# Attention values with the value chunks stationary and four probability columns streaming, in steps of half a head

## The chip, the cores and the metric

The kernel runs on one core of a Trainium2 chip. The metric is the device time of one execution in microseconds (us). The time before is a median of 359.21 us over three runs (358.72 to 359.83). Ratios are computed as the mean time of one kernel's fast runs over the mean of the other's fast runs of the same rounds, so they are not quite the ratio of the medians quoted beside them. A run counts as slow when it is more than 1.5% above the fastest of the same kernel.

## The reference, cut to what matters

Two identical layers for four sequences (B = 4) at decode, so one new token each: an attention block with a cached key and value store of 4096 positions (32 query heads, 8 key/value heads, head size 128), then a gated feed-forward of width 1792.

```python
x = A_x
for _ in range(2):                                   # cut: written out twice in the reference
    h = layernorm(x)
    q = h @ wq                                       # 512 -> 32 heads x 128
    p = softmax(q k^T / sqrt(128))                   # 4 query heads share one key/value head
    x = x + (p v) @ wo
    h = layernorm(x)
    x = x + (gelu(h @ w_gate) * (h @ w_up)) @ w_down
```

The cache is 128 MiB in principle for two layers' worth of reads, but the transposed keys of one sequence stay on chip for both layers. What is loaded is 32 MiB of keys, twice 32 MiB of values, and 13.25 MiB of weights: 114.56 MB.

## The kernel before

For each sequence b, the kernel runs layer 1, and layer 2 up to the softmax. The value products of layer 2 ("the second pass") of sequence b - 1 are interleaved with the work of sequence b. Keys and values come through one ring of six 512 KB buffers, all issued from one queue in program order. A tile is half a head of keys or values.

```python
KV_BUFS = 6
kvin  = tc.tile_pool(name="kvin",  bufs=KV_BUFS)     # the ring, 4 KB per partition and buffer
prp   = tc.tile_pool(name="prp",   bufs=1)
ps_ot = tc.tile_pool(name="ps_ot", bufs=1, space=PSUM)
# ... cut

class Values:                                        # two heads at a time
    def step(self):                                  # half of two heads: two tiles
        # ... cut: two loads v_t into the ring
        for n in range(4):
            hi, k2 = n // 2, n % 2
            for i in range(2):                       # head
                for par in range(2):                 # four row groups of ot
                    kk = 2 * k2 + par
                    r = ZW * (2 * i + par)
                    c = ZW * (2 * (self.pp % 2) + i) + 2 * rep * kk
                    nc.tensor.matmul(self.ot[r:r + 2 * rep, 0],
                                     lhsT=self.pT[:, 2 * t + hi, c:c + 2 * rep],   # 8 columns stay
                                     rhs=vt[i][:, hi, 2 * kk:2 * kk + 2],          # 256 stream
                                     start=(t == 0 and n == 0), stop=(t == 1 and n == 3))
        if t == 1:
            nc.scalar.copy(out=self.os, in_=self.ot[:, 0])
    def finish(self):                                # fp32 selection: sum the wanted rows, transposed
        for k in range(2):
            nc.tensor.matmul(od, lhsT=self.os[:, k, :], rhs=sel[:, k], start=(k == 0), stop=(k == 1))
        nc.vector.tensor_tensor(out=o_bf[...], in0=od, in1=self.rden[...], op=ALU.mult)

# the end of sequence b; W() takes one step of the second pass of sequence b - 1
for n, _ in enumerate(ffn(b, 1)):                    # 3 x 56 pairs of one moving column
    if n > 0: W()
W()
run(layer_norm(b, 1, pad=True))
W()
qs = q_rows(b, 0)
W()
q_turn(qs, 0)
qs = q_rows(b, 1)
sc = scores(0, zq2)
q_turn(qs, 1)
soft2 = [softmax(sc), softmax(scores(1, zq2))]
W()
# then the keys of sequence b + 1
```

Of the kernel before, what the change touches and what calls it, by code (L numbers as in the profile page):

```python
# [1 line left out]

# [5 lines left out]
FP32 = mybir.dt.float32  # L8
BF16 = mybir.dt.bfloat16
I32 = mybir.dt.int32  # L10
ACT = mybir.ActivationFunctionType
ALU = mybir.AluOpType
AX = mybir.AxisListType
RED = bass_isa.ReduceOp
P = 128
# [3 lines left out]
GH = 4  # L19
# [5 lines left out]
def kernel(  # L25
# [41 lines left out]
    prp = ctx.enter_context(tc.tile_pool(name="prp", bufs=1))  # L67
    pTp = ctx.enter_context(tc.tile_pool(name="pTp", bufs=2 * NG))
    osp = ctx.enter_context(tc.tile_pool(name="osp", bufs=1))
# [4 lines left out]
    ps_ot = ctx.enter_context(tc.tile_pool(name="ps_ot", bufs=1, space=bass.MemoryType.PSUM))  # L74
# [20 lines left out]

    sel = const.tile([P, 2, 2, rep], FP32, name="sel")
    idv = ident_f.rearrange("p (s q b h) -> p q b s h", s=2, q=2, h=rep)
    for kbp in range(2):
        nc.vector.tensor_tensor(out=sel[:, kbp], in0=idv[:, 0, kbp], in1=idv[:, 1, kbp],
                                op=ALU.add)  # L100
# [33 lines left out]
    ot_ps = [ps_ot.tile([P, 2, 2 * Dh], FP32, name=f"ot{i}") for i in range(2)]  # L134
    for o in ot_ps:
        nc.vector.memset(o[:], 0.0)

# [96 lines left out]
    def run(gen):  # L234
        for _ in gen:
            pass

    def ffn(b0, nb):

        bs = slice(b0, b0 + nb)  # L240
        yield from layer_norm(b0, nb)
        yield
        h = ps_misc.tile([P, 2, KF, nb], FP32, name="h", tag="misc")
        rb = rstd[:, None, bs].to_broadcast([P, KF, nb])
        for m in range(KF):
            for k in range(KD):
                nc.tensor.matmul(h[:, 0, m, :], lhsT=wg_sb[:, k, m * P:(m + 1) * P],
                                 rhs=xc_bf[:, bs, k], start=(k == 0), stop=(k == KD - 1))
        g_sb = small.tile([P, KF, nb], FP32, name="g_sb", tag="g_sb")
        nc.vector.tensor_tensor(out=g_sb[:], in0=h[:, 0], in1=rb, op=ALU.mult)  # L250
        t1 = small.tile([P, KF, nb], FP32, name="t1", tag="t1")
        nc.vector.tensor_tensor(out=t1[:], in0=g_sb[:], in1=g_sb[:], op=ALU.mult)
        nc.vector.tensor_scalar(out=t1[:], in0=t1[:], scalar1=0.044715, scalar2=1.0,
                                op0=ALU.mult, op1=ALU.add)
        nc.vector.tensor_tensor(out=t1[:], in0=t1[:], in1=g_sb[:], op=ALU.mult)
        th = small.tile([P, KF, nb], FP32, name="th", tag="th")
        nc.scalar.activation(out=th[:], in_=t1[:], func=ACT.Tanh, scale=GELU_C)
        nc.vector.scalar_tensor_tensor(out=g_sb[:], in0=g_sb[:], scalar=0.5, in1=rb,
                                       op0=ALU.mult, op1=ALU.mult)
        nc.vector.scalar_tensor_tensor(out=th[:], in0=th[:], scalar=1.0, in1=g_sb[:],  # L260
                                       op0=ALU.add, op1=ALU.mult)
        yield
        for m in range(KF):
            for k in range(KD):
                nc.tensor.matmul(h[:, 1, m, :], lhsT=wu_sb[:, k, m * P:(m + 1) * P],  # L265
                                 rhs=xc_bf[:, bs, k], start=(k == 0), stop=(k == KD - 1))
        yield
        H_bf = small.tile([P, KF, nb], BF16, name="H_bf", tag="H_bf")
        nc.vector.tensor_tensor(out=H_bf[:], in0=th[:], in1=h[:, 1], op=ALU.mult)
        yT = ps_misc.tile([P, nb, KD], FP32, name="yT2", tag="misc")  # L270
        for dk in range(KD):
            for k in range(KF):
                nc.tensor.matmul(yT[:, :, dk], lhsT=wd_sb[:, k, dk * P:(dk + 1) * P],  # L273
                                 rhs=H_bf[:, k, :], start=(k == 0), stop=(k == KF - 1))
        nc.vector.tensor_tensor(out=XT[:, bs], in0=XT[:, bs], in1=yT[:], op=ALU.add)
# [76 lines left out]
    ot_ctr = [0]  # L352

    class Values:



        def __init__(self, b, pp, prob, o_bf):
            self.b, self.pp, self.o_bf = b, pp, o_bf
            self.pT, self.rden = prob  # L360
            self.ot = ot_ps[ot_ctr[0] % 2]
            ot_ctr[0] += 1
            self.t = 0

        def step(self):
            t = self.t
            self.t += 1
            vt = []
            for i in range(2):
                v = kvin.tile([P, 2, NKB, Dh], BF16, name="v_t", tag="kv")  # L370
                rows = slice(t * CH * P, (t + 1) * CH * P)
                dq.dma_start(out=v.rearrange("p i k d -> p (i k) d"),  # L372
                             in_=A_v_cache[self.b, 2 * self.pp + i, rows].rearrange(
                                 "(p c) d -> p c d", p=P))
                vt.append(v)
            for n in range(4):
                hi, k2 = n // 2, n % 2
                for i in range(2):
                    for par in range(2):
                        kk = 2 * k2 + par  # L380
                        r = ZW * (2 * i + par)
                        c = ZW * (2 * (self.pp % 2) + i) + 2 * rep * kk
                        nc.tensor.matmul(self.ot[r:r + 2 * rep, 0],  # L383
                                         lhsT=self.pT[:, 2 * t + hi, c:c + 2 * rep],
                                         rhs=vt[i][:, hi, 2 * kk:2 * kk + 2].rearrange(
                                             "p k d -> p (k d)"),
                                         start=(t == 0 and n == 0), stop=(t == 1 and n == 3),
                                         skip_group_check=True)
            if t == 1:
                self.os = osp.tile([P, 2, Dh], FP32, name="os", tag="os")  # L390
                nc.scalar.copy(out=self.os.rearrange("p b d -> p (b d)"), in_=self.ot[:, 0])  # L391

        def finish(self):
            od = self.ot[:, 1, 0:2 * rep]
            for k in range(2):
                nc.tensor.matmul(od, lhsT=self.os[:, k, :],  # L396
                                 rhs=sel[:, k].rearrange("p s h -> p (s h)"),
                                 start=(k == 0), stop=(k == 1))
            i0 = self.pp * 2 * rep
            s0 = 2 * (self.pp % 2)  # L400
            nc.vector.tensor_tensor(out=self.o_bf[:, self.b, i0:i0 + 2 * rep], in0=od,  # L401
                                    in1=self.rden[:, s0:s0 + 2].rearrange("p s h -> p (s h)"),
                                    op=ALU.mult)
# [20 lines left out]
    NPP = Hkv // 2  # L424

    def second_pass(b, probs):

        late = []
        for pp in range(NPP):
            v = Values(b, pp, probs[pp // 2], OT2_bf)  # L430
            for t in range(2):
                v.step()
                if late:
                    late.pop()()
                if t == 1:
                    late.append(v.finish)
                yield
        late.pop()()
        yield

    soft2 = prob2 = None
    for b in range(B):
# [3 lines left out]
        def W(n=1):  # L446
            for _ in range(n):
                next(todo, None)
# [11 lines left out]
        else:  # L460
# [3 lines left out]
            keys(b, 1)  # L464
            prob2.append(turn(soft2[1]))
            todo = second_pass(b - 1, prob2)
            keys(b, 2)
# [4 lines left out]
        p1 = turn(soft1)  # L472
        v = [Values(b, pp, p1, OT_bf) for pp in range(2)]
        v[0].step()
        keys(b, 6)
        v[0].step()
        keys(b, 7)
        v[1].step()
        soft1 = softmax(scores(1, z1))
        v[0].finish()  # L480
        if b == 0:
            dma_weights("wo")
        v[1].step()
        p1 = turn(soft1)
        v += [Values(b, pp, p1, OT_bf) for pp in range(2, 4)]
        v[2].step()
        v[1].finish()
        out_proj(b, 1, OT_bf, [0])
        v[2].step()
        out_proj(b, 1, OT_bf, [1, 2])  # L490
        v[3].step()
        v[2].finish()
        out_proj(b, 1, OT_bf, [3])
        v[3].step()
        if b == 0:
            dma_weights("wg", "wu", "wd")
        out_proj(b, 1, OT_bf, [4, 5])
        v[3].finish()
        W()
        out_proj(b, 1, OT_bf, [6, 7])  # L500
        W()
        for n, _ in enumerate(ffn(b, 1)):
            if n > 0:
                W()
        W()
        run(layer_norm(b, 1, pad=True))
        W()
        qs = q_rows(b, 0)
        W()
        q_turn(qs, 0)  # L510
        qs = q_rows(b, 1)
        sc = scores(0, zq2)
        q_turn(qs, 1)
        soft2 = [softmax(sc), softmax(scores(1, zq2))]
        W()
    prob2 = [turn(sf) for sf in soft2]
    todo = second_pass(B - 1, prob2)
    for n, _ in enumerate(todo):
        if n in (3, 5, 7):
            out_proj(0, B, OT2_bf, [n - 3, n - 2])  # L520
    out_proj(0, B, OT2_bf, [6, 7])
# [40 lines left out]
```

## Time and profile before

| | before |
|---|---|
| time, median of 3 | 359.21 us |
| mean load rate over the span | 322 GB/s |
| best slices of the span | 413 to 416 GB/s |
| PE busy | 272.8 us of 357.6 |

First lines of the page: the span, the busy time of each engine, the load rate in GB/s over 40 slices of 8.9 us, and the queue that brings instructions (packets, MB, share).

```profile
span 357.6 us, 10270 instructions
...
PE 272.8 (76%) x4548; PEld 197.1 (55%) x4548; DVE 124.2 (35%) x456; ACT 77.8 (22%) x122; POOL 13.4 (4%) x36
...
GB/s 286 416 416 277 356 356 394 416 396 396 88 169 323 344 406 384 374 376 369 161 312 345 413 400 387 386 380 191 298 359 395 351 369 393 345 265 140 405 47 2
...
q8 instruction: 35, 0.57, 0.6%
```

The rate touches 416 GB/s, but the slices that begin near 89, 170 and 241 us and the last ones fall well below it. The next view puts numbers on these stretches. Its columns are the stretch, the busy time and the instruction count of each engine, the granted clock, the DMA share and the rate.

```profile
core 0: us, PE busy (x) PEld busy (x) DVE busy (x) ACT busy (x) POOL busy (x), PEclk, DMA share, GB/s
90.00:110.00 20.00, 17.12 (x224) 10.59 (x217) 10.70 (x29) 6.78 (x10) 1.65 (x4) 0.82 0.42 149
165.00:190.00 25.00, 22.26 (x336) 15.02 (x329) 13.96 (x35) 10.00 (x14) 2.04 (x5) 0.92 0.77 277
240.00:265.00 25.00, 21.29 (x331) 15.64 (x331) 16.07 (x40) 11.31 (x16) 2.48 (x6) 0.99 0.79 280
312.00:328.00 16.00, 12.31 (x184) 6.36 (x176) 5.55 (x20) 2.30 (x6) 1.66 (x4) 0.82 0.53 194
```

These are the boundaries between sequences: feed-forward done, query rows, scores and softmax of layer 2, first keys of the next sequence. No tile of the ring is used up there for several microseconds, so the queue runs dry: after sequence 1 the last value step ends at 167.20 us and the key transposes begin at 174.32, and from 172 to 176 us the loads ran at 19 GB/s, a DMA share of 0.05.

The groups of the value products (line, engine, operation, tiles, shapes, count; then busy us and mean ns; then idle time before):

```profile
L383 PE MATMUL ot<-v_t,pT 128*8 128x256 bf16 x1024 | 69.1, 369 | 38.5 <-DMA v_t<-in_A_v_cache_dram 31.7
...
L391 ACT COPY os<-ot 128x256 f32<-128x256 f32 x32 | 11.9, 372 | 134.3 <-PE ot L383 134.3
...
L396 PE MATMUL ot<-sel,os 128*128 128x8 f32 x128 | 29.4, 340 | 0.0
```

The last fence of this section is the timeline of PE in a feed-forward stretch (start, duration, engine, line, what, count), and below it the sum of one such stretch, from the gate projection to the query rows of sequence 1, in the columns of the boundary table.

```profile
152.88 1.63 PE L247 MATMUL h<-xc_bf,wg_sb 128*128 128x1 bf16 x56
154.44 1.23 PE L383 MATMUL ot<-v_t,pT 128*8 128x256 bf16 x16
155.60 1.65 PE L265 MATMUL h<-xc_bf,wu_sb 128*128 128x1 bf16 x56
...
158.14 1.02 PE L396 MATMUL ot<-sel,os 128*128 128x8 f32 x4
```

```profile
153.00:164.50 11.50, 11.38 (x247) 8.60 (x248) 3.73 (x24) 0.96 (x3) 0.00 (x0) 0.50 1.02 380
```

PE is busy for 11.38 of 11.50 us there at a clock of 0.50. A pair step of values (L383 x16) takes about 1.0 us there, and so does a selection group (L396 x4).

### The profile page before, as it was taken

The numbers are of one execution on the slowest core, as the hardware profiler recorded it, in microseconds if no ns is written. First come the engines' busy times: TensorE is split into PE (matmuls) and PEld (weight loads), VectorE is DVE, ScalarE is ACT, GpSimd is POOL, SyncE is SP. The second block draws the span as 40 slices with busy tenths as digits, with TensorE's granted clock in tenths as the row PEclk, the third lists the DMA queues.
The fourth block names the chain that finished last, engine by engine and source line by source line (L and its number), as shares of the span: only waits on it lengthen the run. The fifth ranks groups of instructions, "written<-read, shape, count | busy, mean of one in ns | idle before, by whom it ended". The sixth has DMA issues, their size and how long they took to land.

```text
span 357.6 us, 10270 instructions
## 1 busy us (share of the span) xinstructions
PE 272.8 (76%) x4548; PEld 197.1 (55%) x4548; DVE 124.2 (35%) x456; ACT 77.8 (22%) x122; POOL 13.4 (4%) x36
## 2 busy tenths in 40 slices
PE   3777651964888588899887669998876797994785
PEld 3675540654266465584666546755665465742465
DVE  7235230031365430223666211336661203232013
ACT  2325220000055430000346210002562101011000
POOL 0000000000010000000100000001000000001000
PEclk9999885555599985555999975559998755587555
DMA  7997999999259999999489999995899999973910
GB/s 286 416 416 277 356 356 394 416 396 396 88 169 323 344 406 384 374 376 369 161 312 345 413 400 387 386 380 191 298 359 395 351 369 393 345 265 140 405 47 2
DMA packets 35740, 115.22 MB, mean 322 GB/s; under 512 B 3176, under 2 KB 9072, under 8 KB 35696
## 3 DMA queue, kind: packets, MB, share of 16 engines
q1 hardware_dynamic: 35696, 114.58, 85.2%
q8 instruction: 35, 0.57, 0.6%
q14 instruction: 9, 0.07, 0.1%
HBM read 114.56 MB, written 0.00 MB: 320 GB/s over the span
## 4 chain that ended last, share of the span: by engine, by line
PE 39%; DMA 38%; DVE 10%; ACT 6%; issue 2%; SPq 2%; POOL 2%; POOLq 0%; ACTq 0%; DVEq 0%
DMA v_t<-in_A_v_cache_dram 24%; PE ot L383 10%; PE tp L303 8%; PE sc L313 7%; DMA wd_sb<-in_B_w_down_dram 5%; DMA k_t<-in_A_k_cache_dram 5%; DMA wq_sb<-in_A_wq_dram 4%; ACT kt L287 4%; PE ot L396 4%; PE qr L202 4%; DVE kt L289 2%; ACT pr L331 2%; DVE m L320 2%; PE yT L228 2%; SPq L372 2%
## 5 line engine op out<-in xcount | busy, mean ns | idle before, releaser
L383 PE MATMUL ot<-v_t,pT 128*8 128x256 bf16 x1024 | 69.1, 369 | 38.5 <-DMA v_t<-in_A_v_cache_dram 31.7
L303 PE MATMUL tp<-ident_bf,k_t 128*128 128x128 bf16 x1024 | 75.2, 236 | 9.7 <-DVE kt L289 3.7
L303 PEld LDWEIGHTS <-k_t 128*128 128x128 bf16 x1024 | 68.6, 107 | 17.9 <-issue 11.4
L287 ACT COPY kt<-tp 128x1024 bf16<-128x1024 bf16 x52 | 51.9, 1012 | 63.0 <-PE tp L303 62.8
L289 DVE COPY kt<-tp 128x1024 bf16<-128x1024 bf16 x76 | 51.2, 687 | 38.2 <-PE tp L303 37.8
L383 PEld LDWEIGHTS <-pT 128*8 128x8 bf16 x1024 | 27.7, 99 | 58.1 <-issue 41.5
L391 ACT COPY os<-ot 128x256 f32<-128x256 f32 x32 | 11.9, 372 | 134.3 <-PE ot L383 134.3
L313 PE MATMUL sc<-kt,zq 128*32 128x512 bf16 x512 | 34.5, 396 | 4.8 <-DVE zq L214 2.2
L396 PEld LDWEIGHTS ot<-sel,os 128*128 128x128 f32 x128 | 26.5, 289 | 11.4 <-issue 9.7
L396 PE MATMUL ot<-sel,os 128*128 128x8 f32 x128 | 29.4, 340 | 0.0
L401 DVE TENSOR_TENSOR OT_bf<-ot,rden 128x8 bf16<-128x8 f32 x32 | 5.2, 164 | 66.9 <-PE ot L396 66.7
L313 PEld LDWEIGHTS <-zq 128*32 128x32 bf16 x512 | 15.9, 100 | 18.5 <-issue 4.3
L228 PEld LDWEIGHTS <-wo_sb 128*128 128x128 bf16 x640 | 20.9, 107 | 6.8 <-issue 6.8
L228 PE MATMUL yT<-OT_bf,wo_sb 128*128 128x1 bf16 (+1 forms) x640 | 20.7, 166 | 0.7 <-DVE OT_bf L401 0.7
L331 ACT ACTIVATE pr<-sc,nb 128x512 bf16<-128x512 f32 x16 | 11.0, 689 | 44.3 <-DVE am L327 43.4
L320 DVE TENSOR_REDUCE m<-sc 128x1 f32<-128x512 f32 x16 | 10.8, 676 | 25.7 <-PE sc L313 25.7
L325 POOL PARTITION_ALL_REDUCE gm<-am x16 | 6.2, 386 | 283.2 <-DVE am L322 252.9
L202 PE MATMUL qr<-wq_sb,xpad 128*32 128x512 bf16 x128 | 13.6, 570 | 0.5 <-DVE msq L162 0.5
L347 PE MATMUL ptp<-ident_bf,pr 128*128 128x128 bf16 x64 | 6.4, 224 | 8.2 <-ACT pr L331 7.8
L273 PE MATMUL yT<-H_bf,wd_sb 128*128 128x1 bf16 (+1 forms) x280 | 8.2, 166 | 3.8 <-DMA wd_sb<-in_B_w_down_dram 3.5
L273 PEld LDWEIGHTS <-wd_sb 128*128 128x128 bf16 x280 | 8.5, 106 | 4.0 <-DMA wd_sb<-in_B_w_down_dram 3.6
L265 PE MATMUL h<-xc_bf,wu_sb 128*128 128x1 bf16 (+1 forms) x280 | 8.2, 165 | 2.4 <-DMA wu_sb<-in_B_w_up_dram 1.9
(70 smaller groups left out, 138.2 us busy)
## 6 DMA issues: line engine op xcount, KB each, us to landing
v_t<-in_A_v_cache_dram SPq DMA_DIRECT2D x128, 512.0 KB, 6.4
k_t<-in_A_k_cache_dram SPq DMA_DIRECT2D x64, 512.0 KB, 5.6
wq_sb<-in_A_wq_dram SPq DMA_DIRECT2D x2, 2048.0 KB, 12.2
wo_sb<-in_A_wo_dram SPq DMA_DIRECT2D x1, 4096.0 KB, 19.3
wg_sb<-in_B_w_gate_dram SPq DMA_DIRECT2D x1, 1792.0 KB, 10.4
wu_sb<-in_B_w_up_dram SPq DMA_DIRECT2D x1, 1792.0 KB, 14.5
wd_sb<-in_B_w_down_dram SPq DMA_DIRECT2D x1, 1792.0 KB, 19.1
x_bf<-in_A_x_dram SPq DMA_DIRECT2D x1, 4.0 KB
```

The costliest lines, as they stand in the source:

```text
L202: nc.tensor.matmul(qr[ZW * j:ZW * (j + 1), :], lhsT=xpad[:, k, :], rhs=wq_sb[:, k, c0:c0 + rep * Dh], start=(k == 0), stop=(k == KD - 1), ...
L228: nc.tensor.matmul(OP["y"][:, :, dk], lhsT=wo_sb[:, i, dk * P:(dk + 1) * P], rhs=o_bf[:, bs, i], start=(i == 0 and dk == 0), stop=(i == Hq ...
L273: nc.tensor.matmul(yT[:, :, dk], lhsT=wd_sb[:, k, dk * P:(dk + 1) * P], rhs=H_bf[:, k, :], start=(k == 0), stop=(k == KF - 1))
L287: nc.scalar.copy(out=out_ap, in_=in_ap)
L289: nc.vector.tensor_copy(out=out_ap, in_=in_ap)
L303: nc.tensor.transpose(tp[:, kb, :], kn[:, hi, kb, :], ident_bf[:, :])
L313: nc.tensor.matmul(sc[ZW * s:ZW * (s + 1), :], lhsT=zq[:, off:off + ZW], rhs=KT[kvh][:, kb].rearrange("p c k -> p (c k)"), start=(kb == 0) ...
L320: nc.vector.tensor_reduce(out=m[:], in_=sc[:], axis=AX.X, op=ALU.max)
L331: nc.scalar.activation(out=pr.rearrange("p c k -> p (c k)"), in_=sc[:], func=ACT.Exp, bias=nb[:, 0:1], scale=scale, accum_out=ls[:])
L383: nc.tensor.matmul(self.ot[r:r + 2 * rep, 0], lhsT=self.pT[:, 2 * t + hi, c:c + 2 * rep], rhs=vt[i][:, hi, 2 * kk:2 * kk + 2].rearrange("p ...
L391: nc.scalar.copy(out=self.os.rearrange("p b d -> p (b d)"), in_=self.ot[:, 0])
L396: nc.tensor.matmul(od, lhsT=self.os[:, k, :], rhs=sel[:, k].rearrange("p s h -> p (s h)"), start=(k == 0), stop=(k == 1))
```

## The change

Its intent: drop the fp32 selection groups and their copies by letting the 128x128 value chunk stay in the array while the four probability columns of its head stream, so that the sum over chunks happens in PSUM and comes out transposed already; release the ring one tile at a time; split gate and up over two PSUM banks; and place the tiles of the second pass more finely, with the two query groups back to back.

```diff
-    class Values: ...                      # two heads, step of two tiles, finish with selection
+    def values(b, kvh, prob, o_bf):
+        pT, rden = prob
+        s = kvh % GH
+        ot = ps_ot.tile([P, rep], FP32, name="ot", tag="ot")
+        for t in range(2):
+            v = kvin.tile([P, 2, NKB, Dh], BF16, name="v_t", tag="kv")
+            # cut: load of half a head
+            for hi in range(2):
+                for kb in range(NKB):
+                    c = ZW * s + rep * kb
+                    nc.tensor.matmul(ot[:], lhsT=v[:, hi, kb, :], rhs=pT[:, 2 * t + hi, c:c + rep],
+                                     start=(t == 0 and hi == 0 and kb == 0),
+                                     stop=(t == 1 and hi == 1 and kb == NKB - 1))
+            if t == 0:
+                yield
+        nc.vector.tensor_tensor(out=o_bf[:, b, kvh * rep:(kvh + 1) * rep], in0=ot[:],
+                                in1=rden[:, s], op=ALU.mult)
+        yield
# cut: sel and ot_ps removed, prp and ps_ot to 2 buffers, up projection into its own bank hu
-        for n, _ in enumerate(ffn(b, 1)):
-            if n > 0:
-                W()
-        W()
-        run(layer_norm(b, 1, pad=True))
-        W()
-        qs = q_rows(b, 0)
-        W()
-        q_turn(qs, 0)
-        qs = q_rows(b, 1)
-        sc = scores(0, zq2)
-        q_turn(qs, 1)
-        soft2 = [softmax(sc), softmax(scores(1, zq2))]
-        W()
+        for _ in ffn(b, 1):
+            W(2)                           # W(n): n tiles
+        W(2)
+        for _ in layer_norm(b, 1, pad=True):
+            W(1)
+        W(1)
+        qs = q_rows(b, 0), q_rows(b, 1)
+        W(1)
+        q_turn(qs[0], 0)
+        sc = scores(0, zq2)
+        q_turn(qs[1], 1)
+        W(1)
+        soft2 = [softmax(sc), softmax(scores(1, zq2))]
+        late = todo                        # what is left goes between the next keys
# cut: the first pass taken by half heads in the same way
```

## The prediction

> **What bounds the kernel now.** The page shows 114.6 MB loaded in a 357.6 us span: mean 322 GB/s, while the best slices reach 413 to 416. At 410 GB/s the bytes need 279 us; some 77 us are lost. The stretches show where: 90 to 110 us runs at 149 GB/s (12.7 us lost), 165 to 190 at 277 (8.1), 240 to 265 at 280 (7.9), 312 to 345 (13.4), 345 to 358 at 2 (13). Elsewhere the DMA share is about 1.0. In the chain of work that ended last, value loads hold 24% and PE 39%. So the kernel is DMA-bound with a hole at each batch boundary, where no buffer of the six-deep ring comes free: in the timeline the last value step of batch 1 ends at 167.2 us, the first key tile is released at about 175 us, and the queue is empty from 172 to 176. Just before, 152 to 168 us, PE is always busy, at a granted clock of 0.5.
>
> **Removed.** 32 fp32 selection groups (128 matmuls): each took 0.95 us cold, 0.55 warm, about 28 us of PE; 32 ACT copies (11.9 us busy); a gate/up wait of 0.5 us on DVE.
>
> **Added.** 2048 load-and-multiply pairs for 1024. Pairs like them (128x128 bf16 stationary, 1 to 4 columns) went at 1.48 us per 56 (26 ns) to 0.95 us per 32 (30 ns) at clock 0.5, and 1.87 us per 64 at clock 1.0. A 512 KB tile then costs an estimated 0.45 us at either clock; now it is 0.51 us cold and 0.30 warm. Values: about 57 us for 52; PE net about 20 us less, mostly in the cold FFN stretches.[...]
>
> **Moved.** Steps release one tile instead of two, and a tile no longer waits for its pair (the timeline shows 2 matmuls, a wait, then 14). The second pass's last tiles move behind the query rows and scores, one into the next batch's keys.
>
> **On the critical path.** With PE slack in the FFN stretch, DMA is the pace until the boundary, so the ring is still in flight when the chain queries-scores-keys (about 6 us) begins, and covers most of it. I expect the holes at 165 and 240 us to give 3 to 5 us each, the one at 312 us 2 to 4, the first (no second pass to move) 1; the tail 2 to 3; saturated stretches 1 to 2. Sum 12 to 20 us, less a few for keys at a lower clock: 359 to 344 us.
>
> **Predicted: 344 us, 335 to 353.** Faster by over 2%: 0.75; within 2%: 0.20; slower by over 2%: 0.05.
>
> **What would show it.** 16 value pairs in 0.42 to 0.5 us whatever the clock; no fp32 selection group; DMA share above 0.85 in the two middle boundaries (0.77 to 0.79 now); the stretch from 90 to 110 us much as now; mean rate about 335 GB/s; last value landing to end of span 2 us shorter.
>
> **What would make it wrong.** (1) [...]32 key transposes took 2.0 us at clock 1.0 and 3.3 us at a low clock. [...]here FFN stretches run at 0.5 and key stretches at 0.9 to 1.0. If keys went cold too, PE would bind and the gain vanish. (2) The pairs cost 60 ns, not 28: PE +60 us. (3) The boundary is not covered because the late value tiles hold buffers; gain then only 4 to 6 us. (4) Saturated stretches are capped near 380 GB/s.

The cost of a pair rests on the pairs measured in the trace before.

## The result, and the profile after

| | before | after |
|---|---|---|
| time, median of 3 | 359.21 us | 355.35 us (355.05 to 356.29) |
| ratio to before, fast runs | | 0.9897, interval 0.9859 to 0.9935 |
| span of the profiled run | 357.6 us | 354.5 us |

The kernel is faster by 1%, where 4% was forecast, and the time lies just above the stated range. Two later calls ran the same kernel again as a control: ratios of 0.9909 and 0.974. The sign is safe; the size varies between about 1 and 2.6%.

The same lines of the page after:

```profile
span 354.5 us, 12013 instructions
...
PE 247.8 (70%) x5444; PEld 200.6 (57%) x5444; DVE 127.4 (36%) x484; ACT 66.0 (19%) x90; POOL 13.4 (4%) x36
...
GB/s 279 411 407 279 349 354 389 407 399 375 184 159 337 329 412 383 409 396 291 197 355 350 410 295 406 408 327 196 232 394 368 392 359 411 383 275 129 398 176 2
...
q8 instruction: 42, 0.69, 0.8%
```

PE has 25 us less to do (247.8 for 272.8), as forecast (20). The mean rate rose only from 322 to 325 GB/s. The instruction queue moved 0.69 MB for 0.57. The four boundaries, in the same stretches as before:

```profile
90.00:110.00 20.00, 17.57 (x243) 11.21 (x244) 12.51 (x36) 7.93 (x11) 1.65 (x4) 0.88 0.54 187
165.00:190.00 25.00, 21.58 (x365) 16.14 (x362) 15.56 (x40) 12.15 (x16) 2.48 (x6) 0.97 0.86 299
240.00:265.00 25.00, 22.01 (x336) 15.67 (x334) 14.38 (x39) 11.03 (x15) 2.48 (x6) 0.90 0.77 270
312.00:328.00 16.00, 11.42 (x264) 7.49 (x256) 5.98 (x25) 1.56 (x4) 1.65 (x4) 0.82 0.50 179
```

In the same columns as before: the middle two, on which the forecast rested, went from 277 to 299 GB/s and from 280 down to 270 (events come up to 3 us earlier after, so the stretches match only roughly). Of the signs that the prediction named, the DMA share passed 0.85 in one of the two middle boundaries only (0.86 and 0.77), the mean rate reached 325 GB/s of about 335, and the stretch from 90 to 110 us, which was to stay, rose from 149 to 187 GB/s. The groups:

```profile
L356 PE MATMUL ot<-pT,v_t 128*128 128x4 bf16 x2048 | 69.8, 166 | 48.2 <-DMA v_t<-in_A_v_cache_dram 36.8
...
L361 DVE TENSOR_TENSOR OT_bf<-ot,rden 128x4 bf16<-128x4 f32 x64 | 10.1, 158 | 81.0 <-PE ot L356 80.9
```

The selection groups and copies are gone. The value pairs ran at the cost that was forecast: in the chain of work that ended last, 16 of them took 0.41 to 0.60 us, the longer figures with the whole record of the last matmul (166 ns in the mean), for an estimate of 0.45.

So nothing in the sum of costs was missed on the side of PE's work. What is new is idle time. This is PE's list of waits (who waited, for what, us in total, times, longest):

```profile
PE ot L356 <- DMA v_t<-in_A_v_cache_dram: 36.8, 45, 10.7
...
PE ot L356 <- issue: 4.7, 3, 1.8
...
PE yT L264 <- issue: 2.6, 1, 2.6
...
PE hu L256 <- issue: 1.8, 2, 1.1
PE yT L218 <- issue: 1.2, 2, 0.9
```

"Issue" is time in which the engine waited for nothing that the profile shows. In the trace before, PE's list has no such entry at all. The timeline of the same feed-forward stretch shows where it sits: in the middle of a run of pairs, with operands long in place.

```profile
151.85 0.19 PE L256 MATMUL hu<-xc_bf,wu_sb 128*128 128x1 bf16 x2
152.78 1.60 PE L256 MATMUL hu<-xc_bf,wu_sb 128*128 128x1 bf16 x54 [0.74 <-issue]
154.24 0.99 PE L356 MATMUL ot<-pT,v_t 128*128 128x4 bf16 x32
155.09 1.26 PE L264 MATMUL yT<-H_bf,wd_sb 128*128 128x1 bf16 x42
158.98 0.54 PE L264 MATMUL yT<-H_bf,wd_sb 128*128 128x1 bf16 x14 [2.63 <-issue]
```

```profile
149.50:161.70 12.20, 8.75 (x298) 8.42 (x296) 2.55 (x18) 0.21 (x1) 0.00 (x0) 0.50 0.92 348
```

The stretch from the gate projection to the query rows is the place where PE slack was forecast. PE was busy for only 8.75 us instead of 11.38, and the stretch still grew from 11.5 to 12.2 us, and its load rate fell from 380 to 348 GB/s.

The packet records of the trace tell what PE waited for. The instruction queue moves packets of 16,384 bytes: 35 before, for 9,096 matmuls and loads of PE, and 42 after, for 10,888. So the 7 packets more came with 1,792 instructions more, 256 to a packet. Taking idle times of 0.25 us or more that end on "issue", the kernel after has eight, 10.4 us together, all within feed-forward or output-projection stretches. Every one of them ended 1.2 to 1.6 us after such a packet had landed. The one of 2.63 us began at 156.35 us; a packet began at 156.4 us, took 1.02 us, and PE went on at 158.98 us, 1.55 us after it landed. Runs of pairs at 26 to 30 ns use up 256 instructions (128 pairs) in an estimated 3.3 to 3.8 us.

Counting PE's instructions (matmuls, loads and the 12 semaphore and drain instructions) in the trace's order gives a sharper test. All eight stalls sit at the same place of the count, to within one: 193 past a multiple of 256, and so do all 96 stalls of this kind in the fifteen traces that have any. So they fall at one place of every 256 instructions, called a seam below, and nowhere else. Most seams pass without one (34 of 42 here). Three times a second stall came exactly 256 instructions after a first one, 3.56 to 3.58 us later. In each stall, 2.2 to 2.6 us passed from the start of the packet to PE's next matmul. What makes a packet start too late stays open. A packet at 98.3 us, with no data load under way (DMA share 0.02 from 97.4 to 100.4 us), took 1.10 us, as long as those before the stalls (1.02 to 1.11), so full DMA engines are not shown to be the reason.

One more thing is visible. The scores at the boundary ran at the full clock in one sequence and at half of it in another; these are two lines of the chain of work that ended last, the same 32 matmuls:

```profile
166.53 1.94 PE sc L304 x32
...
240.59 3.63 PE sc L304 x32
```

The granted clock was 1.00 in the first of these and 0.50 in the second. Where no clock is given below, "half clock" and "full clock" of a score group are read from its length against these two.

Finally the time between the starts of the query rows of successive sequences (from the timelines): 75.8, 72.8 and 74.6 us before; 71.8, 74.1 and 74.9 after. So the gain of about 4 us in the first was partly given back in the others (1.3 and 0.3). From the last value matmul to the last copy of the output: 12.0 us before, 9.3 after.

### The profile page after: what moved, and what is told of

Same layout as the page of the kernel before. It is cut to its first block, busy times and chain, and to the rows that moved or that the text cites. A ratio compares the mean times of both kernels' runs of the same rounds, so it can differ in the third digit from the quotient of the medians.

```text
span 354.5 us, 12013 instructions
## 1 busy us (share of the span) xinstructions
PE 247.8 (70%) x5444; PEld 200.6 (57%) x5444; DVE 127.4 (36%) x484; ACT 66.0 (19%) x90; POOL 13.4 (4%) x36
## 4 chain that ended last, share of the span: by engine, by line
DMA 39%; PE 34%; DVE 12%; ACT 6%; issue 5%; POOL 2%; SPq 2%; ACTq 0%; POOLq 0%; DVEq 0%
DMA v_t<-in_A_v_cache_dram 18%; DMA k_t<-in_A_k_cache_dram 10%; PE tp L294 8%; PE sc L304 8%; PE ot L356 7%; DMA wd_sb<-in_B_w_down_dram 6%; DMA wq_sb<-in_A_wq_dram 5%; PE qr L192 4%; ACT kt L278 3%; DVE kt L280 3%; ACT pr L322 3%; PE yT L264 2%; DVE m L311 2%; PE hu L256 1%; SPq L351 1%
## 5 line engine op out<-in xcount | busy, mean ns | idle before, releaser
L356 PE MATMUL ot<-pT,v_t 128*128 128x4 bf16 x2048 | 69.8, 166 | 48.2 <-DMA v_t<-in_A_v_cache_dram 36.8
L356 PEld LDWEIGHTS <-v_t 128*128 128x128 bf16 x2048 | 63.7, 103 | 57.9 <-DMA v_t<-in_A_v_cache_dram 42.0
L304 PE MATMUL sc<-kt,zq 128*32 128x512 bf16 x512 | 37.1, 414 | 5.3 <-DVE zq L204 2.1
L361 DVE TENSOR_TENSOR OT_bf<-ot,rden 128x4 bf16<-128x4 f32 x64 | 10.1, 158 | 81.0 <-PE ot L356 80.9
L304 PEld LDWEIGHTS <-zq 128*32 128x32 bf16 x512 | 14.0, 102 | 21.9 <-issue 6.3
L247 ACT ACTIVATE th<-t 128x14 f32<-128x14 f32 (+1 forms) x5 | 1.1, 222 | 109.7 <-DVE t L245 109.7
L218 PEld LDWEIGHTS <-wo_sb 128*128 128x128 bf16 x640 | 19.5, 104 | 1.9 <-issue 1.9
L256 PE MATMUL hu<-xc_bf,wu_sb 128*128 128x1 bf16 (+1 forms) x280 | 8.5, 165 | 4.8 <-DMA wu_sb<-in_B_w_up_dram 2.9
L256 PEld LDWEIGHTS <-wu_sb 128*128 128x128 bf16 x280 | 8.0, 104 | 5.0 <-DMA wu_sb<-in_B_w_up_dram 3.0
L338 PEld LDWEIGHTS <-pr 128*128 128x128 bf16 x64 | 4.5, 103 | 9.7 <-ACT pr L322 8.9
```

The costliest lines, as they stand in the source:

```text
L218: nc.tensor.matmul(OP["y"][:, :, dk], lhsT=wo_sb[:, i, dk * P:(dk + 1) * P], rhs=o_bf[:, bs, i], start=(i == 0 and dk == 0), stop=(i == Hq ...
L256: nc.tensor.matmul(hu[:, m, :], lhsT=wu_sb[:, k, m * P:(m + 1) * P], rhs=xc_bf[:, bs, k], start=(k == 0), stop=(k == KD - 1))
L304: nc.tensor.matmul(sc[ZW * s:ZW * (s + 1), :], lhsT=zq[:, off:off + ZW], rhs=KT[kvh][:, kb].rearrange("p c k -> p (c k)"), start=(kb == 0) ...
L338: nc.tensor.transpose(ptp[:, cc, :], pr[:, cc, :], ident_bf[:, :])
L356: nc.tensor.matmul(ot[:], lhsT=v[:, hi, kb, :], rhs=pT[:, 2 * t + hi, c:c + rep], start=(t == 0 and hi == 0 and kb == 0), stop=(t == 1 and ...
```

## The experiments

The theories. F: PE starves for instructions in dense runs of short pairs, and that ate the slack. Rivals: O, the new order is at fault, as late value tiles hold the ring at the boundary; T, the PE time of the pairs themselves binds; R, the depth of the ring binds whatever PE does; A, whatever lean64 gains comes from better value steps and a better clock, not from instructions.

Sixteen kernels ran; the ratios are to the kernel before, run on the same chip. "Correct" has a limit here: lean64 and half4 leave out or falsify half of the value products and still passed the comparison, presumably since the attention output is small beside x, which no run shows. Only lean_ffn failed it.

### Fewer instructions in the value steps: lean64 and half4

```diff
-                for kb in range(NKB):
+                for kb in range(0, NKB, 2):
-                    nc.tensor.matmul(ot[:], lhsT=v[:, hi, kb, :], rhs=pT[:, 2 * t + hi, c:c + rep], ...)
+                    nc.tensor.matmul(ot[:], lhsT=v[:, hi, kb, :], rhs=pT[:, 2 * t + hi, c:c + 64], ...)   # lean64 only
```

> Wrong result on purpose: half of the value pairs, each with 64 moving columns in place of 4, so 2048 fewer PE instructions at about the same PE time per tile at the low clock[...]. Theory F (PE starves for instructions: the changed kernel shows 8 idle times of 0.3 to 2.6 us put down to issue, 10.4 us together, each ending 1.2 to 1.6 us after a 16 KB packet of the instruction queue landed; the kernel before shows none): these idle times go, and the time falls to 345 to 350 us. Theory O (the new order is at fault: late value tiles hold the ring at the batch boundary): 354 to 356, as the changed kernel.

> Wrong result on purpose: half of the value pairs, 4 moving columns: 2048 fewer PE instructions and about 28 us less PE time. Theory F: no issue idle, and within 3 us of lean64. Theory T (the PE time of the pairs themselves is what binds): at least 5 us below lean64. Theory O: 352 to 356.

lean64: median 344.65 us, ratio 0.9593 (0.9506 to 0.968). The issue idle fell from 10.4 us in eight places to 2.4 in three, and the query rows came every 70.5, 70.0 and 69.7 us. A pair of 64 columns took 53 ns in this trace (from one start to the next, at half clock), so eight of them take an estimated 0.42 us, for the 0.45 estimated for 16 pairs of four columns. half4: median 346.32 us (340.09 to 347.87), three of four runs classed slow, so there is no ratio; issue idle 3.2 us. This is nearly what theory F asked for (some idle time is left), and O is refuted as the whole cause: the order was left as it was. half4 is not below lean64 in the median, but its one fast run is, so T is not excluded by it. lean64 is also not a clean test: at the high clock its value steps are shorter too (0.39 to 0.41 us between the keys, for 0.54 to 0.56 in the kernel after at a granted clock of 1.00). A cleaner one follows below (lean_ffn).

### Form and order apart: newform_oldorder and oldform_neworder

newform_oldorder keeps the order of before and replaces only the products:

```diff
     def step(self):                        # still two tiles
-        for n in range(4): ...             # 16 matmuls of 256 columns in four row groups
+        for i in range(2):
+            for hi in range(2):
+                for kb in range(NKB):
+                    nc.tensor.matmul(self.ot[:, i], lhsT=vt[i][:, hi, kb, :], rhs=self.pT[..., c:c + rep], ...)
     def finish(self):
-        # selection matmuls
         nc.vector.tensor_tensor(out=o_bf[...], in0=self.ot, in1=self.rden[...], op=ALU.mult)
```

oldform_neworder keeps the old class and takes its steps at every other place of the new order. It also splits gate and up over two banks, and to find room it takes three transposed-probability buffers and builds the identity in a ring buffer, two of the economies of ring6c below.

> Correct result: the new value products (stationary value chunks, four columns) in the order of the kernel before (steps of two tiles, same places). Theory F: issue idle of 5 to 12 us is there too, the time is 352 to 358 us. Theory O: without the new order the full gain appears, 344 to 349 us.

> Correct result: the old value products and fp32 selection groups at the places of the new order (two tiles at every other place). Theory F: no issue idle; PE time as before, so 355 to 360 us: the order alone gives little. Theory O (the order costs something): 360 to 366 us.

| | old order, two tiles a step | new order |
|---|---|---|
| old products | 1 | 0.9971 (0.9873 to 1.0068), two tiles a step |
| new products | 1.0123 (1.0039 to 1.0206) | 0.9897 (0.9859 to 0.9935), one tile a step |

The new products alone make the kernel slower, although they take 22 us off PE's busy time (251.1 us): 363.69 us, with 9.3 us of issue idle in six places. The order alone shows no clear effect (358.58 us, no issue idle), though its smaller buffers could hide a gain: ring6c, with these and two more economies, lay about 5 us above the changed kernel. Only together do they gain, where a step also holds one tile instead of two. O expected 344 to 349 for the first and is refuted again. T is refuted as well: PE had less to do and the kernel was slower. F's numbers held in the second and missed by 6 us in the first (363.69 for 352 to 358). All four score groups at the boundaries of that kernel were slow (2.1 to 2.7 us from first to last start, for 1.5 at full clock), so a lower clock may have a part in its loss.

### Where the tiles of the second pass go: spread and all_early

```diff
# spread: W(1) between all parts of the feed-forward, query rows and scores, two tiles late
-        for _ in ffn(b, 1):
-            W(2)
-        W(2)
+        for n, _ in enumerate(ffn(b, 1)):
+            W(2 if n == 0 else 1)
+        W(1)
...
-        qs = q_rows(b, 0), q_rows(b, 1)
+        qs = [q_rows(b, 0)]
+        W(1)
+        qs.append(q_rows(b, 1))
# all_early: one more W(1) before and one more after the query rows, none after the scores
```

> Correct result: the changed kernel with the same instructions, but the second pass's 16 tiles spread over feed-forward, query rows and scores (six in the feed-forward and five between the query rows and scores, two left late) in place of nine or so in a dense run. Theory F: broken by query rows and scores, the dense runs of short pairs are shorter, the issue idle falls from 10.4 us to under 5, and the batch boundary is filled: 344 to 350 us. Theory O (late tiles hold the ring): more tiles late, so 356 or more.

> Correct result: the changed kernel with all 16 tiles of the second pass ahead of the scores, none late. Theory F: denser runs of short pairs, issue idle as much or more than 10.4 us, the same time or up to 5 us more: 355 to 360. Theory O: the boundary opens, 349 to 353 us.

spread: 356.05 us, ratio 0.985 (0.9761 to 0.9939), issue idle still 8.7 us in seven places. My expectation missed: output projections and feed-forward are dense enough runs of short pairs without the value tiles. all_early: two slow and two fast runs (350.5 to 359.16), ratio 0.9781 (0.9668 to 0.9894), issue idle 7.7 us; inconclusive between the theories. Neither differs clearly from the changed kernel, so nothing shows that the late tiles, a risk that the prediction named, ate the gain. The two fast runs of all_early (350.5 and 354.5) leave room for 2 to 3 us.

### Fewer instructions in the feed-forward alone: lean_ffn, with a control

```diff
-            for k in range(KD):
-                nc.tensor.matmul(hg[:, m, :], lhsT=wg_sb[:, k, ...], rhs=xc_bf[:, bs, k], ...)
+            for k in range(0, KD, 2):
+                nc.tensor.matmul(hgw[:, m * nb:m * nb + 64], lhsT=wg_sb[:, k, ...], rhs=wq_sb[:, k, 0:64], ...)
# the same for up and down
```

> The changed kernel once more, as the control of this call: 353 to 357 us, issue idle of 8 to 12 us in 6 to 9 places, ratio to the kernel before 0.98 to 0.995.

> Wrong result on purpose: value products untouched; the feed-forward uses half the pairs with 64 moving columns each, so 840 fewer PE instructions, about 210 per batch, at about the same PE time at the low clock (an estimate: 84 x 53 ns = 4.5 us per batch for 168 x 27 ns = 4.5). Theory F (instruction starvation in the feed-forward stretch costs time by itself): issue idle under 5 us and 348 to 352 us. Rival A (lean64 was faster because its value steps and its clock were better, not for the starvation): 353 to 357 us, as the control, even with the idle gone.

The 53 ns were measured in lean64, the 27 ns are those of the one-column pairs in the trace before (1.48 us per 56).

The control: 354.29 us, ratio 0.9909 (0.9854 to 0.9964), issue idle 9.4 us. lean_ffn: 349.1 us, ratio 0.9735 (0.9668 to 0.9801), issue idle 2.4 us. PE's list of waits of lean_ffn has these issue entries left, and its feed-forward stretch of sequence 1 is this:

```profile
PE yT L218 <- issue: 1.4, 3, 0.7
...
PE ot L364 <- issue: 1.0, 1, 1.0
```

```profile
149.60:160.10 10.50, 9.17 (x223) 8.73 (x223) 2.90 (x20) 0.22 (x1) 0.00 (x0) 0.50 1.03 407
```

PE's busy time did not fall (251.5 us for 248.2 in the control), the value steps are untouched, and the stretch that took 12.2 us in the kernel after takes 10.5 us at 407 GB/s. That is the slack that was forecast, and it appears once PE no longer waits for instructions. Its worth, from this pair: 5.2 us by the medians. Rival A is refuted for that part. Two differences remain. The gate and up pairs of lean_ffn read a weight tile, so they no longer wait for the normalised input; in the kernel after these waits came to 1.1 us. And the clock: the profiles of both have one boundary after sequences 1 to 3 with scores at half clock, so that does not tell them apart.

The loads around the query rows of sequence 1 show what the stalls did: first the 2 us before these start, then the 22 us from their start. The lines are from the kernel before, the kernel after and lean_ffn, in this order.

```profile
162.45:164.45 2.00, 1.90 (x18) 1.30 (x17) 1.57 (x11) 0.00 (x0) 0.00 (x0) 0.50 1.06 371
164.45:186.45 22.00, 19.47 (x288) 12.62 (x291) 11.93 (x30) 7.80 (x11) 1.65 (x4) 0.90 0.73 258
...
159.69:161.69 2.00, 1.96 (x60) 1.87 (x57) 0.93 (x8) 0.00 (x0) 0.00 (x0) 0.50 0.53 119
161.69:183.69 22.00, 19.32 (x307) 12.79 (x311) 13.29 (x40) 7.53 (x10) 1.65 (x4) 0.89 0.83 282
...
158.08:160.08 2.00, 1.54 (x36) 1.44 (x36) 0.83 (x7) 0.00 (x0) 0.00 (x0) 0.50 1.02 404
160.08:182.08 22.00, 19.93 (x323) 13.14 (x320) 13.04 (x38) 7.53 (x10) 1.66 (x4) 0.90 0.80 292
```

The loads ran down just before the query rows in the kernel after (119 GB/s) and did not in lean_ffn (404). In the 22 us that follow, even lean_ffn gains little over the kernel before: 292 for 258 GB/s here, 273 for 268 and 247 for 238 after sequences 2 and 3. At 410 GB/s that is an estimated 0.3 to 1.8 us a boundary.

### Depth of the ring: ring7, ring6c, ring5, ring7_lean64

A seventh buffer needs 4 KB more per partition. ring7 takes it from other pools, and ring6c makes the same economies with six. The 1.3 us that the expectations give to a tile are 512 KB at 410 GB/s.

```diff
-KV_BUFS = 6
+KV_BUFS = 7                                # ring6c: 6
-    prp = ctx.enter_context(tc.tile_pool(name="prp", bufs=2))
-    pTp = ctx.enter_context(tc.tile_pool(name="pTp", bufs=2 * NG))
+    prp = ctx.enter_context(tc.tile_pool(name="prp", bufs=1))
+    pTp = ctx.enter_context(tc.tile_pool(name="pTp", bufs=3))
# cut: identity built in a ring buffer, one zq1 tile instead of two
```

> Correct result: the changed kernel with seven buffers in the ring in place of six (room made by one probability buffer, three transposed-probability buffers and one query tile). Theory F: the issue idle stays and delays releases; a seventh tile covers 1.3 us more of each of three boundaries, at most 4 us: 351 to 354 us. Theory R (ring depth is what binds at the boundary): 5 to 9 us less: 346 to 350.

> Correct result: control for ring7: the same smaller buffers with six in the ring. All theories: as the changed kernel, 353 to 357 us; if it is slower by 2 us or more, the room that ring7 needs costs that much.

> Wrong result on purpose: ring of seven and the 64-column half-count value pairs together. If a deeper ring only absorbs the starvation stalls, the two do not add: 342 to 347 us. If ring depth and starvation are separate losses, they add: 335 to 341 us.

> Correct result: the changed kernel with five buffers in the ring. If ring depth binds in this kernel at every boundary and stall (7 to 10 us gained by the seventh): 8 to 14 us more, 363 to 370. If only the boundary holes see it (three holes of 1.3 us each): at most 5 us more, 355 to 360.

| | median us | ratio to before | issue idle us |
|---|---|---|---|
| ring7 | 350.9 | 0.9734 (0.9663 to 0.9805) | 13.8 |
| ring6c | 360.72 | 1.0003 (0.992 to 1.0086) | 8.6 |
| ring7_lean64 | 340.21 | 0.9485 (0.9409 to 0.956) | 2.4 |
| ring5 | 371.39 | 1.0383 (1.0319 to 1.0446) | 4.4 |

One tile of depth is worth 9.8 us between ring6c and ring7, and 17 us between ring5 and the control of its call; both are more than theory F allowed, so the ring is a loss of its own. The issue idle is largest of these four in ring7 and yet that kernel is fast: this suggests that a stall of PE costs time only as far as the loads in flight do not bridge it. ring7_lean64 lies in the range for adding losses: 4.4 us under lean64, 10.7 under ring7 by medians. They were run at other times. ring6c was itself 5 us above the changed kernel, for its smaller buffers; which one of them is answered only in part below. The clock is a rival for a part of both figures: in the profile of ring6c the first score group after each of sequences 1 to 3 was at half clock, in that of ring7 and that of the kernel after only one of three, and the timelines put one such boundary at about 2 us.

### Does the ring bind the old kernel too: before_ring5, with ring7 beside the changed kernel

```diff
-KV_BUFS = 6                                # in the kernel before
+KV_BUFS = 5
# ring7b: ring7 with pr in two buffers, one query tile, query groups one after the other
```

> The changed kernel, as the control of this call: 353 to 357 us.

> Correct result: ring7 beside the changed kernel on one chip: 349 to 353 us, 0.985 to 0.99 of the control.

> Correct result: seven buffers in the ring, two probability buffers as in the changed kernel, and one query tile with the query groups taken one after the other (room from one padded query tile, a shared feed-forward tile and a one-batch attention output). ring6c was about 5 us above the changed kernel for its smaller buffers. If that price was the single probability buffer: 344 to 348 us. If it was the single query tile with both query groups ahead of it: also 344 to 348, as the order is mended. If it was the three transposed-probability buffers: 349 to 353, as ring7.

> Correct result: the kernel before with five buffers in the ring, against ring5 which cost the changed kernel 17 us. If the changed kernel leans on the ring more than the old one did (stalls of PE that only the ring can bridge): the old one loses at most 8 us, 360 to 367. If ring depth binds both alike: 15 to 20 us, 374 to 380; or more, as the old one holds two tiles at a time.

| | median us | ratio to before |
|---|---|---|
| after_third | 353.34 | 0.974 (0.9687 to 0.9793) |
| ring7_again | 348.71 | 0.9662 (0.9601 to 0.9722) |
| ring7b | 351.87 | 0.9692 (0.9622 to 0.9762) |
| before_ring5 | 391.79 | 1.0804 (1.0761 to 1.0847) |

Taking a buffer away costs the old kernel 30 us and the changed one 17. So both lean on the ring, and the old one more; my guess that the stalls make the new one lean harder fell. That the old one uses up and frees two tiles at a time, and holds the first while it waits for the second, is the likely reason, though no run takes that alone apart. It fits the table of form and order, where the new products at two tiles a step lost.

ring7 is the best correct version: 2.7 to 3.4% under the kernel before. Against the changed kernel it is 4.6 us lower in the median, but the intervals of the two ratios overlap. In the profiles of this pair no score group after sequences 1 to 3 is at half clock, so these 4.6 us are the cleaner figure for the seventh buffer with its economies. ring7b was no better than ring7, so the price of the smaller buffers is not simply the single probability buffer; that stays open (its profile, of a slow run, has half-clock scores at all four boundaries).

## Why the prediction was wrong

The forecast was 344 us, 335 to 353; it came to 355.35.

- **What bounds the kernel: right.** Loads, with holes at the boundaries. The ring runs agree: 17 us for one buffer taken away.
- **Work removed and added: right.** PE lost 25 us (20 forecast). 16 pairs took 0.41 us at best (0.45). Selection groups and copies gone.
- **The tail: right.** 12.0 to 9.3 us from the last value matmul to the output (2 to 3 us forecast). Since the whole gain in the span was 3.1 us, this tail is nearly all of it; gains and losses ahead of it cancelled.
- **The first boundary: better than forecast.** From the query rows of sequence 0 to the first scores of sequence 1 the time fell from 21.9 to 19.5 us (1 us forecast): the query groups now run back to back, and the first 32 score matmuls that followed took 1.65 us from first to last start instead of 2.99. These 1.3 us, at a granted clock of 0.93 instead of 0.50, were not forecast.
- **The middle boundaries: wrong. This is the step that failed:** "With PE slack in the FFN stretch, DMA is the pace until the boundary, so the ring is still in flight when the chain queries-scores-keys (about 6 us) begins, and covers most of it. I expect the holes at 165 and 240 us to give 3 to 5 us each, the one at 312 us 2 to 4". The slack was counted in busy time, and PE's busy time did fall there, from 11.38 to 8.75 us. But the stretch grew, since PE stood without instructions for 3.4 us in it (0.74 and 2.63), and the loads ran down before the boundary: 119 GB/s in the last 2 us, for 371 in the kernel before. lean_ffn removed most of that idle time with PE's work kept, and gave 5.2 us. A second term of the same step was too large by itself: with the loads at 404 GB/s up to the query rows, as forecast, the ring still did not cover "most of" the chain. The 22 us from the query rows on gained an estimated 0.3 to 1.8 us in lean_ffn, for 3 to 5 or 2 to 4 forecast. Part of the reason may be the chain's length: in the kernel before, the query rows start at 164.45 us and the keys at 174.32, so it takes 9.9 us and not about 6. The kernel before took its 35 packets of instructions without any idle time of this kind; with the 42 of the kernel after there were 10.4 us of it.
- **Risk (1), the clock: half right.** Key stretches stayed mostly at 0.9 to 1.0 (1.00 from 171.2 to 192 us and from 247 to 268 in the kernel after). But at the boundaries after sequences 1 to 3 the first score group, 1.5 us from first to last start at full clock, took 2.0 to 3.0 us in 15 of 30 cases in the ten fast profiles that have the full count of new value pairs, in one of nine (2.05 us) in the three with the old products, and in none of six in lean64 and ring7_lean64. In the kernel after and its first control, one boundary each was so: 22.0 and 21.7 us from the query rows to the next scores, where the others of these two took 19.2 to 20.1, so about 2 us. after_third, the control with the largest gain, had none. This is seen, not tried alone: no run changed the clock and nothing else, and why the new pairs should decide it is open. A busy PE alone did not bring the full clock: the feed-forward stretch of the kernel before had PE busy for 11.38 of 11.50 us at a granted clock of 0.50.
- **Risk (2), the cost of a pair, and risk (4), a cap near 380 GB/s: neither.** Pairs ran at 26 to 30 ns (the 60 of the risk was an assumption), though the record of one load alone is 103 ns in the mean, and lean_ffn loaded at 407 GB/s in the stretch where the kernel before had 380.
- **Risk (3), the late tiles: not shown.** all_early and spread moved them either way with no clear difference.
- **What is left open.** lean64 lies 4.5 us below lean_ffn. It was run at another time. Shorter value steps at the high clock, the warm boundaries, and its fewer instructions in the output projections all differ; they were not taken apart.

The size of the missing term: the forecast left about 15 us of gain, the trace shows about 4; instruction starvation takes 5 of the missing 11 by lean_ffn, half-clock scores about 2 by the timelines (the kernel before had one such group too, at its first boundary), and the rest is not assigned; the boundaries that stay open in lean_ffn are where to look.

## What to carry to other kernels

When a change trades few long instructions for many short ones, count instructions as a resource that is loaded like data: here runs of load-and-multiply pairs at 27 ns used up 16 KB of instructions in 3.6 us, and PE idled at the seams where its busy time said it had slack. Where idle time looks causeless, count instructions between the stops: a constant step of 256 gave the cause away here. Read "issue" idle in the list of waits, and compare the length of a stretch, not its busy time. And in a kernel bound by loads, look at the depth of the ring first: one more buffer gave 4.6 us beside the changed kernel and 9.8 beside ring6c, about as much as the whole change with its 25 us less engine work (3.9, 4.6 and 8.7 us). Freeing a tile as soon as it is used is likely depth without memory, but no run tried it alone.
